# Rows of V for a sparse attention: a gathering engine's indirect DMAs replaced, for four of six query tiles, by copies from register addresses on another queue, and the output stores moved the other way

## The chip, the cores and the metric

The kernel runs on one core of one Trainium2 chip. The metric is the device time of one execution in microseconds (us), median of several runs. A run is put in the state "slow" when it is over 1.5% above the fastest run of the same kernel in its set; such runs are left out of every ratio, and a single run has state "unknown". "Span" is the time from the first to the last instruction of the one execution that the profiler recorded; it is about 2 us shorter than the device time.

The runs fell on several chips, numbered 2, 8, 9 and 10 here. A kernel's ratio is always to the kernel before on the same chip and in the same set; where two sets are set side by side below, it is by their ratios or their traces.

Engines: TensorE (PE in the profile) multiplies matrices, VectorE (DVE) and ScalarE (ACT) do elementwise work, Pool (POOL, GpSimd) issues indirect DMAs and does some gathers itself, and SyncE (SP) mainly issues DMAs. Each takes its instructions in program order, as the queues in the traces below show.

## The reference

A block-sparse attention (768 positions, blocks of 32, 8 heads, 4 batches) followed by a feed-forward stage. Each middle block of queries sees the first and last block, its neighbours, and three sampled blocks.

```python
def _attn_ref(q, k, v, sampled_blocks):
    ...
    mask = np.abs(blk_i - blk_j) <= window          # window = 1
    mask = mask | (blk_i == 0) | (blk_j == 0) | (blk_i == n_blocks - 1) | (blk_j == n_blocks - 1)
    for qb in range(n_blocks):                      # 24 blocks
        for kb in sampled_blocks[qb]:               # 3 of them for each
            mask[qb*block:(qb+1)*block, kb*block:(kb+1)*block] = True
    ...                                             # softmax over the mask, then attn @ v

def _moe_ref(x, w_in, w_out, g_ln):                 # x: 3072 x 512
    h = x @ w_in
    solu = h * softmax(h)                           # (softmax written out in the original)
    ...                                             # layer norm over 1024, times g_ln
    return (ln @ w_out).astype(np.float32)
```

The sampled blocks are data. So the kernel has to fetch, for each block of queries, three blocks of 32 rows of V whose position it learns at run time.

## The kernel before

It works batch by batch, three "tiles" of 256 query rows in each. While batch b is computed, batch b+1 is prepared: V, K and Q are loaded by SyncE, V is cast and written in the order that the gathers want (`place_v`, `write_v`), and the sampled rows are brought in by Pool (`gather_v`). What is prepared when is a table of slots. `at(slot, f)` puts a piece of work in a slot, 24 slots to a batch, and the slots are run in order; since the engines' queues are in order too, a DMA in slot 14 of SyncE goes out behind everything of slots 0 to 13. In particular, what is put in slots 21 to 24 (the second tile's rows) stands ahead of the V loads for the batch after, which begin in slot 24, slot 0 of the next batch.

```python
def load_one(src, b, pr, nm, ...):                  # V, K and Q of one pair of heads
    ...
    nc.sync.dma_start(out=..., in_=src[b, 2*pr : 2*pr+2, :, :]...)      # buffers: kc 3, qc 2, vc 2

def place_v(b, i):                                  # cast to bf16 into vst, on DVE or ACT
    ...
    if b and i % 2:
        nc.scalar.copy(out=dst, in_=src)
    else:
        nc.vector.tensor_copy(out=dst, in_=src)

def near_v(b, t): ...                               # neighbours' rows, two DMAs on SyncE

def gather_v(b, g):                                 # sampled rows of two query blocks
    for i in range(2):
        qb = 2 * g + 1 + i
        nc.gpsimd.indirect_dma_start(               # 96 rows of 1040 bytes
            out=vr[0 : NR * BLK, g, i, :], out_offset=None, in_=v_s[b][:, :],
            in_offset=bass.IndirectOffsetOnAxis(ap=vidx[0 : NR * BLK, qb : qb + 1], axis=0))

def rows_v(t):                                      # 24 row numbers into SyncE registers
    q0, n_ = 8 * t + 1, min(8, NM - 8 * t)
    _, at_row[t] = nc.values_load_multi_w_load_instructions(
        vrow[0:1, :, q0 : q0 + n_], engines=(mybir.EngineType.SP,), ...)

def fetch_v(b, g):                                  # the same rows, 32 at a time, on SyncE
    ...
    for i in range(2):
        for j in range(NR):
            r = at_row[t][j * n_ + 2 * (g - 4 * t) + i]
            nc.sync.dma_start(out=vr[j * BLK : (j + 1) * BLK, g, i, :],
                              in_=v_s[b][bass.ds(r, BLK), :])

def store(b, t, ot):
    ...
        nc.sync.dma_start(out=out[r0 : r0 + n, :], in_=ot[p0 : p0 + n, :])

def plan(b):                                        # what batch b + 1 needs; z = 24 * b
    ...                                             # slots for b > 0:
    #   V loads 0, 2, 4, 6   K loads 1, 3, 5, 7   Q loads 9, 11, 12, 14
    #   place_v 3, 5, 7, 9   K casts 5, 7, 9, 11
    for t in range(NT):
        at(z + (13 + o // 4, 21, 28)[t], lambda t=t: near_v(b + 1, t))
        for g in range(4 * t, min(4 * t + 4, NG)):
            at(z + (13 + o // 4, 21, 28)[t] + g - 4 * t, lambda g=g: gather_v(b + 1, g))
```

`rows_v` and `fetch_v` are already there: batch 0 uses them once, for two of its groups (12 copies). A tile has four groups (the third tile three), a group is one call of `gather_v`, which is two indirect DMAs, or of `fetch_v`, which is six copies. So a batch has 22 indirect DMAs.

The softmax here doesn't subtract the row's maximum and nothing guards it: scores larger than these inputs give would overflow.

## Time and profile before

| | |
|---|---|
| device time, three runs | 277.16 us median (275.26 to 280.33) |
| profiled execution (of another run) | 336.05 us, span 334.3 us |
| PE busy, idle gaps over 0.3 us (profiled) | 259.3 us, 68.9 us |
| of these gaps, inside Pool's bursts of indirect DMAs | 33.7 us of 92 us |
| indirect DMAs on Pool | 76: 10 for batch 0, 22 for each other batch |

The profiled execution and the timed ones disagree by 59 us (336.05 against 277.16). That was the riddle. First, lines of the profile's page. "busy" is in us, with the number of instructions after x; the rows of digits are busy tenths in 40 equal slices of the span, PEclk is the clock granted to TensorE in tenths; then the chain of work that ended last, by engine, and one group of instructions (busy us, mean ns of one, idle before it).

```profile
span 334.3 us, 8508 instructions
...
PE 259.3 (78%) x3646; PEld 172.4 (52%) x3646; DVE 173.2 (52%) x491; ACT 148.3 (44%) x216; POOL 124.3 (37%) x122
...
PE   4974976978296779874859959957967959999984
...
POOL 7053672345757520366660230670670140000000
PEclk9799697699759579996787978996985978999999
...
PE 56%; DVE 17%; issue 9%; another core or an unknown queue 7%; ACT 5%; DMA 4%; ACTq 0%; SPq 0%; DVEq 0%
...
L296 POOL DMA_INDIRECT vr<-v_s_125,vidx x22 | 20.8, 946 | 21.5 <-PE op L533 15.4
```

The span is 334.3 us though PE is busy for only 259.3. Pool's indirect DMAs take 0.95 us each in the profile, and Pool's row of digits shows where they come in long bursts.

Next, the timeline of the kernel before inside one of these bursts (start in us, length, engine, line, operation, out<-in, count, and in brackets the idle time before and its releaser):

```profile
151.78 0.92 POOL L296 DMA_INDIRECT vr<-v_s_125,vidx  x1 [0.30 <-issue]
152.47 0.26 PE L631 MATMUL s3p<-onesf,sq 128*128 128x1 bf16 x4 [1.09 <-issue]
...
153.01 0.92 POOL L296 DMA_INDIRECT vr<-v_s_125,vidx  x1 [0.30 <-issue]
153.89 0.25 PE L631 MATMUL s3p<-onesf,sq 128*128 128x1 bf16 x4 [1.16 <-issue]
...
154.24 0.92 POOL L296 DMA_INDIRECT vr<-v_s_125,vidx  x1 [0.30 <-issue]
```

The columns to look at are the start and the count. Between two indirect DMAs of Pool, 1.23 us apart, PE does four tiny matmuls and then stands still for about a microsecond, with "issue" as releaser: nothing that the profile shows held it. I call this the crawl.

### The profile page before, as it was taken

To read this page: it belongs to the slowest core of one execution; us is meant where nothing else is said; L and a number is where in the kernel's file an instruction comes from. 1 tells how busy PE (TensorE), PEld (TensorE's weight loads), DVE (VectorE), ACT (ScalarE), POOL (GpSimd) and SP (SyncE) were. 2 spreads that over 40 slices of the span, in tenths; PEclk is the share of its full clock that TensorE was granted. 3 is DMA by queue.
4 is the path that set the end of the run, shared out by engine and by line. 5 is a ranking of instruction groups with operands and counts; after the bars stand their busy time and mean duration, and the time that the engine had idled before them with its cause. 6 is when DMAs were issued, how large, how long until landed. Compare 5 with 4: busy or idle time off the path is not lost.

```text
span 334.3 us, 8508 instructions
## 1 busy us (share of the span) xinstructions
PE 259.3 (78%) x3646; PEld 172.4 (52%) x3646; DVE 173.2 (52%) x491; ACT 148.3 (44%) x216; POOL 124.3 (37%) x122
## 2 busy tenths in 40 slices
PE   4974976978296779874859959957967959999984
PEld 1442555556153545762337647635544647677752
DVE  7676436599260335682626418517626416364551
ACT  1662557585131245661316427505514325565332
POOL 7053672345757520366660230670670140000000
PEclk9799697699759579996787978996985978999999
DMA  6799679675305951872183290860240130201011
GB/s 211 269 318 147 202 217 305 221 204 186 85 12 152 269 171 40 285 225 66 43 244 94 74 299 23 266 191 23 81 135 26 56 104 3 65 2 65 2 64 64
DMA packets 29734, 46.03 MB, mean 138 GB/s; under 512 B 4296, under 2 KB 22632, under 8 KB 29696
## 3 DMA queue, kind: packets, MB, share of 16 engines
q1 hardware_dynamic: 24976, 34.75, 32.7%
q0 software_dynamic: 4720, 10.74, 12.4%
q8 instruction: 28, 0.46, 0.6%
q14 instruction: 10, 0.08, 0.1%
HBM read 36.76 MB, written 9.77 MB: 139 GB/s over the span
## 4 chain that ended last, share of the span: by engine, by line
PE 56%; DVE 17%; issue 9%; another core or an unknown queue 7%; ACT 5%; DMA 4%; ACTq 0%; SPq 0%; DVEq 0%
PE h L616 14%; PE ops L657 12%; PE op L533 12%; PE s L410 7%; PE s3p L631 4%; DMA vn_128<-v_s_123 3%; PE tp L340 3%; DVE solu L621 2%; DVE w_out_sb L578 2%; ACT ot L663 2%; PE tps L602 1%; DVE xT L605 1%; DVE qr L333 1%; DMA v_s_123<-vst 1%
## 5 line engine op out<-in xcount | busy, mean ns | idle before, releaser
L616 PE MATMUL h<-xT,w_in_sb 128*128 128x256 bf16 x384 | 60.6, 311 | 7.8 <-DVE solu L621 3.1
L657 PE MATMUL ops<-w_out_sb,solu 128*128 128x512 bf16 x192 | 50.8, 400 | 2.1 <-ACT ot L663 1.8
L621 DVE TENSOR_TENSOR solu<-h,e 128x512 bf16<-128x512 f32 x48 | 33.0, 688 | 32.5 <-ACT e L620 24.2
L616 PEld LDWEIGHTS <-w_in_sb 128*128 128x128 bf16 x384 | 39.5, 109 | 19.3 <-issue 9.5
L620 ACT ACTIVATE e<-h 128x512 bf16<-128x512 f32 x48 | 28.6, 597 | 40.1 <-PE h L616 27.5
L481 DVE RECIPROCAL r<-op 128x4 f32<-128x4 f32 x48 | 8.6, 180 | 57.1 <-PE op L533 19.9
L533 PE MATMUL op<-vr,eb 128*32 128x65 bf16 x640 | 20.5, 206 | 16.0 <-issue 16.0
L533 PEld LDWEIGHTS <-ea 64*64 64x64 bf16 (+1 forms) x496 | 18.3, 109 | 21.3 <-issue 9.3
L296 POOL DMA_INDIRECT vr<-v_s_125,vidx x22 | 20.8, 946 | 21.5 <-PE op L533 15.4
L657 PEld LDWEIGHTS <-solu 128*128 128x128 bf16 x192 | 17.8, 101 | 20.8 <-issue 5.4
L296 POOL DMA_INDIRECT vr<-v_s_126,vidx x22 | 20.5, 931 | 20.3 <-PE op L533 14.2
L412 ACT ACTIVATE eb<-s 128x1024 bf16<-128x1024 f32 (+1 forms) x22 | 20.8, 947 | 15.5 <-remote 10.2
L412 ACT ACTIVATE ea<-s 128x1024 bf16<-128x1024 f32 x22 | 22.5, 1021 | 9.1 <-PE op L533 5.5
L663 ACT ACTIVATE ot<-ops,rs 128x512 f32<-128x512 f32 x24 | 16.3, 688 | 22.9 <-PE ops L657 11.3
L410 PEld LDWEIGHTS <-kT 128*64 128x64 bf16 (+1 forms) x316 | 17.0, 112 | 15.5 <-issue 12.6
L412 ACT ACTIVATE ed<-s 128x768 bf16<-128x768 f32 x16 | 12.8, 811 | 26.0 <-PE op L533 9.2
L296 POOL DMA_INDIRECT vr<-v_s_124,vidx x22 | 21.2, 964 | 8.3 <-issue 6.1
L605 DVE COPY xT<-tps 128x512 bf16<-128x512 bf16 x24 | 9.8, 420 | 25.3 <-PE tps L602 12.4
L533 PEld LDWEIGHTS <-eb 128*32 128x32 bf16 x640 | 11.1, 99 | 22.3 <-issue 20.2
L622 DVE TENSOR_TENSOR sq<-solu 128x512 bf16<-128x512 bf16 x48 | 21.1, 442 | 0.9
L482 DVE TENSOR_TENSOR x<-op,r 128x256 bf16<-128x256 f32 x48 | 20.4, 424 | 1.0
L358 ACT COPY kT<-tp 128x768 bf16<-128x768 bf16 x16 | 12.8, 800 | 14.2 <-PE tp L340 14.1
(292 smaller groups left out, 484.6 us busy)
## 6 DMA issues: line engine op xcount, KB each, us to landing
kc<-in_k_dram SPq DMA_DIRECT2D x16, 384.0 KB
qc<-in_q_dram SPq DMA_DIRECT2D x16, 384.0 KB
out_dram<-ot SPq DMA_DIRECT2D x20, 256.0 KB
vc<-in_v_dram SPq DMA_DIRECT2D x12, 384.0 KB
krt_144<-in_moe_w_out_dram POOLq DMA_DIRECT2D x1, 1536.0 KB
w_in_sb<-in_moe_w_in_dram POOLq DMA_DIRECT2D x1, 1024.0 KB
v_s_123<-vst SPq DMA_DIRECT2D x1, 780.0 KB
vn_128<-v_s_123 SPq DMA_DIRECT2D x1, 780.0 KB
```

The source lines that it names most:

```text
L296: nc.gpsimd.indirect_dma_start(out=vr[0 : NR * BLK, g, i, :], out_offset=None, in_=v_s[b][:, :], in_offset=bass.IndirectOffsetOnAxis(ap=vi ...
L410: nc.tensor.matmul(dst, lhsT, rhs, start=(o % 512 == 0), stop=(x == last[o // 512]), skip_group_check=True)
L412: nc.scalar.activation(out=e, in_=s[:, 0:width], func=ACT.Exp, scale=scale)
L482: nc.vector.tensor_tensor(out=xt[:, :, 2 * pr * D : (2 * pr + 2) * D].rearrange("p a (h d) -> p a h d", h=2), in0=op[:, :, :, 0:D], in1=r. ...
L533: nc.tensor.matmul(o_, l_, r_, start=(x == 0), stop=(x == len(mm) - 1), skip_group_check=True)
L616: nc.tensor.matmul(h[:, ff, :], w_in_sb[:, c, f * P : (f + 1) * P], st["xT"][:, c, :], start=(ff == 0 and c == 0), stop=(ff == 1 and c == ...
L620: nc.scalar.activation(out=st["e"][:, sl, :], in_=h, func=ACT.Exp)
L621: nc.vector.tensor_mul(out=st["solu"][:, sl, :], in0=h, in1=st["e"][:, sl, :])
L622: nc.vector.tensor_mul(out=st["sq"][:, sl, :], in0=st["solu"][:, sl, :], in1=st["solu"][:, sl, :])
L631: nc.tensor.matmul(s3p[:, qt, g : g + 1], st[nm][:, f, qt * P : (qt + 1) * P], onesf[:, 0:1], start=first, stop=(qt == 1 and g == 2 and f ...
L657: nc.tensor.matmul(ops, st["solu"][:, f, qt * P : (qt + 1) * P], w_out_sb[:, f, :], start=(f == 0), stop=(f == KF - 1))
L663: nc.scalar.activation(out=ot, in_=ops, func=ACT.Copy, scale=st["rs"][:, qt : qt + 1])
```

## The change

The intent: take load from Pool. For the first two tiles (of 256 rows, four of 128 rows) of batches 1 to 3, the 16 indirect DMAs are replaced by 48 copies of 32 rows, whose addresses SyncE reads from its registers. To make room on SyncE, the stores of the output go to Pool. The third tile stays with Pool. For batches 2 and 3 the first tile moves one slot later (13 to 14).

```diff
@@ store @@
-            nc.sync.dma_start(out=out[r0 : r0 + n, :], in_=ot[p0 : p0 + n, :])
+            nc.gpsimd.dma_start(out=out[r0 : r0 + n, :], in_=ot[p0 : p0 + n, :])
@@ plan @@
         for t in range(NT):
-            g0 = 4 * t
-            at(z + (13 + o // 4, 21, 28)[t], lambda t=t: near_v(b + 1, t))
+            s0 = z + (14, 21, 28)[t]
+            at(s0, lambda t=t: near_v(b + 1, t))
+            if t < NT - 1:
+                at(s0, lambda t=t: rows_v(t))
             for g in range(4 * t, min(4 * t + 4, NG)):
-                at(z + (13 + o // 4, 21, 28)[t] + g - 4 * t, lambda g=g: gather_v(b + 1, g))
+                at(s0 + g - 4 * t, lambda g=g, f=fetch_v if t < NT - 1 else gather_v:
+                   f(b + 1, g))
```

## The prediction

> **What bounds the kernel now.** The page gives PE 259.3 us busy of a profiled span of 334.3; the timed median is 277.16. So the timed program has room for little more than 18 us of TensorE idleness, if the matmuls take there what they take in the profile. The trace has far more: PE gaps over 0.3 us sum to about 69 us. About 34 us of them lie in the stretches (92 us in all) in which Pool issues the indirect DMAs, where PE does a handful of matmuls every 0.72 us (timeline, 149 to 157 us). I read most of this crawl as something of the profiled run. Timed, the kernel is PE-bound in a lock-step of in-order queues, about 20 us per 256-row tile.
>
> **What the change removes.** Per batch 1 to 3, 16 of 22 indirect DMAs: 1.23 us each with the gap (timeline of Pool), 59 us of Pool time in all. Also 28 store issues of 0.35 us from SyncE, and its waits on ACT's output tiles (168 us in SP's waits, harmless unless a load stands behind one).
>
> **What it adds.** On SyncE, for each of two tiles per batch: one load of 24 registers, 5.09 us the one time the trace has it (212 ns a register; the Trainium skill, "Runtime: NRT & Kernel Launch", section "Instruction fetch mechanics", gives about 200), then 24 copies of 32 rows; the undisturbed ones of batch 0 come every 0.50 us. So 17 us per tile and, with the near rows, 36 us per batch, in order, on the queue that also prefetches Q, K and V. Pool gets 28 stores; its two last direct DMAs took 0.74 and 0.91 us, so about 23 us, and its queue now waits for ACT at each.
>
> **How much is critical.** Pool's gathers seldom are when timed: they end well before their reader. SyncE's new work is. In slot order:
> - Fetching for batch 1: after the staging DMA at 68.6 us, near rows, registers and 12 copies precede the third Q load; it goes out about 7 us later than the 73.7 us of now. Estimated stall 6 to 8 us. The next batch's first V load goes out at about 106 us instead of 101.9, while timed slots run faster: another 5 to 7 us.
> - For batch 2: the last Q load waits for slot 16's relay; only then come 36 us of fetches, ending near slot 30, while V placement of the next batch stands in slot 27 on VectorE. Estimated stall 9 us.
> - For batch 3: no loads behind, nothing lost.
> - Last stores from Pool: 1 to 2 us in the tail.
>
> Cost 20 to 25 us. Against it: what of the crawl is real when timed, and Pool's second K gather coming about 10 us sooner: 0 to 20 us. Balance +8 us: 285 us, 262 to 302. Chances: faster by over 2% 0.33, within 2% 0.17, slower 0.50.
>
> **What would show each step.** In the profile after: six more register loads of 5 us and 144 more copies at 0.5 us on SyncE; Pool busy down by about 35 us; V and Q loads behind the fetches later; VectorE and ACT idle ahead of the V placement and the Q casts, ended by a DMA; smaller PE gaps where the gathers were, so the profiled span may fall even where the timed one rises; stores from Pool at 0.7 to 1.0 us.
>
> **What would make it wrong.** The crawl being real when timed: removing two thirds of the gathers is then worth up to 20 us and the change wins. Copies issued faster than 0.50 us, or slots slower than my 2.5 us, hide the SyncE queue. Copies slowed by other transfers, or Pool's K gathers stuck behind store waits, make it worse than 302.

## The result

The changed kernel took 306.52 us (305.90 to 307.30, four runs), the kernel before 277.44 us (275.26 to 280.33, four runs). The ratio is 1.108, with a 95% interval of 1.100 to 1.115: slower by 11%. Ratios in this document are the mean time of one kernel's fast runs over that of the other's fast runs of the same rounds, so they are not quite the ratio of the medians quoted beside them.

The profile after came from an execution of 306.04 us, of the 275 level. The profile of before, by its span and its crawl, is of the 338 level, so the two must not be subtracted from each other. For that reason the kernel before was profiled once more, on chip 9 (the run c2_before_again below: 275.36 us, span 273.6 us). These are the lines of the page after:

```profile
span 304.2 us, 8906 instructions
...
PE 247.5 (81%) x3628; PEld 168.4 (55%) x3646; DVE 174.6 (57%) x491; ACT 148.2 (49%) x216; POOL 95.6 (31%) x102
...
PE   4885677797868996988899916898989999999880
...
POOL 8033776044452350252413500342240712010102
PEclk9799598669965997997999975697879999999997
...
PE 30%; issue 18%; DVE 17%; DMA 14%; SPq 13%; ACT 4%; POOL 1%; POOLq 0%; ACTq 0%; DVEq 0%
PE ops L657 9%; SPq L314 8%; PE op L533 6%; DMA kc<-in_k_dram 6%; PE h L616 5%; SPq L304 4%; PE s L410 3%; DMA vn_128<-v_s_123 3%; PE tp L340 3%; DMA vr<-v_s_123 2%; DVE solu L621 2%; DVE w_out_sb L578 2%; PE s3p L631 2%; DVE qr L333 2%; DVE sq L622 2%
...
L592 POOL DMA_DIRECT2D out_dram<-ot x28 | 16.0, 572 | 103.0 <-ACT ot L663 103.0
```

And these are the same lines of the kernel before at the same level (with one group more at the end):

```profile
span 273.6 us, 8508 instructions
...
PE 232.7 (85%) x3646; PEld 161.0 (59%) x3646; DVE 172.7 (63%) x491; ACT 147.2 (54%) x216; POOL 124.7 (46%) x122
...
PE   5796495598789859959988999999699999999893
...
POOL 8014577407367567746747662576571700000000
PEclk9799889858999968986999999999999999999998
...
PE 55%; DVE 18%; DMA 12%; issue 4%; ACT 4%; SPq 3%; POOL 2%; ACTq 0%; DVEq 0%
...
L296 POOL DMA_INDIRECT vr<-v_s,vidx x76 | 73.0, 961 | 32.8 <-issue 13.2
...
L410 PE MATMUL s<-qbd,krt 128*128 128x64 bf16 x320 | 15.4, 198 | 2.9 <-POOL krt L380 2.8
```

How to read the pair. Pool's busy time has fallen by 29 us (124.7 to 95.6) while PE's idle time and PE's busy time have both risen: the number of matmuls is the same (the trace after lacks 18 of 3646 records), yet they take 247.5 instead of 232.7 us. The rows of PEclk say why: before, the clock is full (9) almost throughout the second half; after, it dips to 5 and 6 in slices 12 and 13 and again in 25 and 26. And in the chain of work that ended last, SyncE's queue (SPq) has grown from 3% to 13%, of which line 314, the new copies, is 8% and line 304, the register load, 4%.

The same kernel before at the 275 level also explains the riddle. This is its timeline inside a burst of indirect DMAs:

```profile
132.10 0.92 POOL L296 DMA_INDIRECT vr<-v_s,vidx  x1 [0.30 <-PE s L410]
...
132.41 0.34 PE L631 MATMUL s3p<-onesf,e 128*128 128x1 bf16 x8 [0.33 <-DVE solu L621]
...
132.61 0.29 PE L631 MATMUL s3p<-onesf,solu 128*128 128x1 bf16 x6
...
132.76 0.68 PE L410 MATMUL s<-qbd,kT 128*128 128x128 bf16 x9
...
133.33 0.96 POOL L296 DMA_INDIRECT vr<-v_s,vidx  x1 [0.30 <-PE s L410]
```

Pool issues them just as fast as in the first profile (0.92 us, 1.23 us apart; mean 961 ns), but PE does 8, 6 and 9 matmuls in the time in which it did 4. Over all of Pool's bursts (93 us) PE's gaps sum to 7.0 us here, 5.4 of them in the head of the kernel, against 33.7 us at the 338 level. So at the level where the times were taken there was almost nothing to win by taking gathers from Pool.

### Where the 30.6 us come from

Comparing the two executions of the 275 level (spans 273.6 and 304.2 us), PE's idle gaps over 0.3 us grow from 36.6 to 51.4 us (+14.8) and PE's busy time by 14.8 us. Together that is 29.6 of the 30.6 us. Cut at the tiles' first outputs, over half of the loss lies in one stretch, 162.7 to 195.6 us, which takes 32.9 us where the kernel before takes 17.0; each of the eight other stretches compared loses at most 3.3 us. The lines below are of that stretch.

**The idle gaps: loads that come late on SyncE.** This is SyncE's queue in the kernel before at the 275 level, as the V loads of batch 3 are issued (SPq lines give when the issue began and how long it took):

```profile
144.07 0.42 SPq L84 DMA_DIRECT2D vc<-in_v_dram  x1
...
145.05 0.47 SPq L84 DMA_DIRECT2D vc<-in_v_dram  x1
...
159.14 0.39 SPq L84 DMA_DIRECT2D vc<-in_v_dram  x1
...
161.71 0.49 SPq L84 DMA_DIRECT2D vc<-in_v_dram  x1
```

And this is the queue of the changed kernel over the same work:

```profile
163.72 12.37 SPq L314 DMA_DIRECT2D vr<-v_s_125  x24
176.14 1.38 SPq L84 DMA_DIRECT2D vc<-in_v_dram  x1
...
178.08 0.47 SPq L84 DMA_DIRECT2D vc<-in_v_dram  x1
...
181.00 0.39 SPq L84 DMA_DIRECT2D vc<-in_v_dram  x1
...
184.35 0.37 SPq L84 DMA_DIRECT2D vc<-in_v_dram  x1
```

In the changed kernel, 24 copies occupy the queue from 163.7 to 176.1 us, half a microsecond each, and behind them stand the V loads: at 176, 178, 181 and 184 us, against 144, 145, 159 and 162 us before. Ahead of the copies of each tile stands a register load too (4.9 to 5.1 us; register loads are not in this view). Those who needed V had to wait, as the changed kernel's timeline shows of the same moment:

```profile
180.40 0.56 DVE L266 CAST vst<-vc 128x768 bf16<-128x768 f32 x1 [3.82 <-DMA vc<-in_v_dram]
...
181.93 0.82 PE L340 MATMUL tp<-ident,kr 128*128 128x128 bf16 x6 [6.14 <-DVE kr L333]
...
183.49 0.83 ACT L264 CAST vst<-vc 128x768 bf16<-128x768 f32 x1 [6.43 <-DMA vc<-in_v_dram]
...
185.60 0.56 DVE L333 CAST kr<-kc 128x768 bf16<-128x768 f32 x1 [3.72 <-DMA kc<-in_k_dram]
```

VectorE stood for 3.8 and 3.7 us, ScalarE for 6.4 us, each ended by a DMA of V or K. Summed after 60 us, such waits on DMA of VectorE and ScalarE are 2.2 us before and 21.5 us after. PE starves with them: its gap from 175.8 us is 6.1 us long (the second line), until VectorE has cast a K that came late. The stores on Pool make no such wait here: after 60 us no wait over 0.3 us of PE, VectorE or ScalarE in this trace ends with Pool or with an output DMA.

**The busy time: half the clock, for the most part around the stalls.** Below are windows of the kernel before at the 275 level; after the engines' busy times come the granted clock of PE, the share of the DMA engines and GB/s.

```profile
80.00:100.00 20.00, 15.41 (x273) 10.96 (x271) 12.96 (x30) 9.03 (x13) 13.41 (x12) 0.94 0.66 187
...
140.00:160.00 20.00, 18.94 (x303) 13.42 (x302) 13.17 (x33) 11.29 (x18) 12.54 (x13) 1.00 0.60 181
...
180.00:200.00 20.00, 17.00 (x300) 12.40 (x298) 15.15 (x37) 11.41 (x18) 12.89 (x13) 1.00 0.46 137
```

The same windows in the changed kernel:

```profile
80.00:100.00 20.00, 15.46 (x191) 10.63 (x190) 10.57 (x23) 7.26 (x12) 7.68 (x6) 0.66 0.43 117
...
140.00:160.00 20.00, 18.41 (x301) 13.40 (x301) 13.96 (x36) 10.55 (x16) 4.95 (x4) 0.91 0.37 100
...
180.00:200.00 20.00, 14.29 (x173) 8.65 (x174) 7.80 (x25) 9.61 (x12) 4.82 (x4) 0.62 0.79 245
```

In the window 180 to 200 us, which the stall at 175.8 runs into, the clock is 0.62 on average: the trace's records of it show half clock for 17.1 us, from 178.3 to 195.4. The window 80 to 100, in which the late Q loads fall, has 0.66. The clock takes only two values here, 1.0 and 0.5, and changes in steps of about 3.4 us. The Trainium skill, "TensorE: Matmul & The Clock Gate", section "What's actually happening", describes two such states: half of the pulses after an idle window of about 3.4 us, all of them after a busy one. This trace agrees in the two values and in the step, but its half-clock stretches do not begin after idle steps alone: in the step before, PE was busy for 23% (at 178.3 us), but also for 59% (at 86.2 and 209.0), 63% (at 222.7) and 80% (at 140.8), while the clock stayed full after steps of 62% and 63% (from 69.1 and 147.6 us). What decides there was not found.

After 60 us, the kernel before spends 19.0 us at half clock and the changed one 56.5 us; PE is busy in 13.1 and 42.2 us of these. Of the 56.5 us, 34.1 begin with PE's gaps at 85.7 us (1.7 us long), 113.8 (2.6) and 175.8 (6.1); 13.7 us (from 140.8, 209.0 and 222.7) have no gap over 1 us just before them, so not all of it is shown to come from the stalls.

Had the 29.1 us of additional half-clock work taken half as long at full clock, PE's busy time would be 14.5 us lower, which is nearly all of the 14.8 us by which it grew (it grew after 60 us only). That is an estimate from these numbers, of the kind that the section "HAM oscillation — how this bites in real kernels" of the same page makes. It is on the high side: in this trace the matmuls of line 657 start 216 ns apart at full clock and 427 at half, but the small ones of line 533 start 26 and 37 ns apart.

**The tail.** The last lines of the changed kernel:

```profile
295.96 1.27 ACT L663 ACTIVATE ot<-ops,rs 128x512 f32<-128x512 f32 x2
296.94 1.60 POOL L592 DMA_DIRECT2D out_dram<-ot  x3 [9.93 <-ACT ot L663]
```

And those of the kernel before at the same level:

```profile
268.67 1.26 ACT L663 ACTIVATE ot<-ops,rs 128x512 f32<-128x512 f32 x2
269.38 1.57 SPq L592 DMA_DIRECT2D out_dram<-ot  x3
```

In the changed kernel the final stores go out at 297 us and the span ends at 304.2: Pool's program ends with a DRAIN (5.49 us, from 297.9), which the busy times don't count. From the last output tile to the end it takes 7.0 us, the kernel before 3.7; PE's final gap is 7.4 us instead of 4.0.

### The profile page after: what moved, and what is told of

Its sections match the earlier page's. It is cut to its first block, busy times and chain, and to the rows that moved or that the text cites. A ratio compares the mean times of both kernels' runs of the same rounds, so it can differ in the third digit from the quotient of the medians.

```text
span 304.2 us, 8906 instructions
## 1 busy us (share of the span) xinstructions
PE 247.5 (81%) x3628; PEld 168.4 (55%) x3646; DVE 174.6 (57%) x491; ACT 148.2 (49%) x216; POOL 95.6 (31%) x102
## 4 chain that ended last, share of the span: by engine, by line
PE 30%; issue 18%; DVE 17%; DMA 14%; SPq 13%; ACT 4%; POOL 1%; POOLq 0%; ACTq 0%; DVEq 0%
PE ops L657 9%; SPq L314 8%; PE op L533 6%; DMA kc<-in_k_dram 6%; PE h L616 5%; SPq L304 4%; PE s L410 3%; DMA vn_128<-v_s_123 3%; PE tp L340 3%; DMA vr<-v_s_123 2%; DVE solu L621 2%; DVE w_out_sb L578 2%; PE s3p L631 2%; DVE qr L333 2%; DVE sq L622 2%
## 5 line engine op out<-in xcount | busy, mean ns | idle before, releaser
L616 PE MATMUL h<-xT,w_in_sb 128*128 128x256 bf16 x384 | 51.7, 281 | 2.6 <-DVE xT L605 1.5
L592 POOL DMA_DIRECT2D out_dram<-ot x28 | 16.0, 572 | 103.0 <-ACT ot L663 103.0
L616 PEld LDWEIGHTS <-w_in_sb 128*128 128x128 bf16 x384 | 35.8, 100 | 9.7 <-issue 3.3
L657 PEld LDWEIGHTS <-solu 128*128 128x128 bf16 x192 | 19.1, 107 | 21.2 <-issue 7.9
L340 PE MATMUL tp<-ident,kr 128*128 128x128 bf16 x96 | 10.0, 254 | 24.5 <-DVE kr L333 23.7
L622 DVE TENSOR_TENSOR sq<-solu 128x512 bf16<-128x512 bf16 x48 | 22.1, 460 | 1.2
L340 PEld LDWEIGHTS <-kr 128*128 128x128 bf16 x96 | 7.0, 112 | 28.2 <-DVE kr L333 26.2
L410 PEld LDWEIGHTS <-kT 128*64 128x64 bf16 (+1 forms) x316 | 16.5, 113 | 10.9 <-issue 7.8
L605 DVE COPY xT<-tps 128x512 bf16<-128x512 bf16 x24 | 9.5, 418 | 13.7 <-PE tps L602 13.6
L533 PE MATMUL op<-vr,eb 128*32 128x65 bf16 x640 | 17.2, 208 | 0.0
L678 PE MATMUL warm<-ident 128*128 128x512 bf16 x42 | 15.2, 471 | 1.5 <-POOL ident L101 1.5
```

The source lines that it names most:

```text
L340: nc.tensor.matmul(tp[:, r, :], c[:, r, :, :].rearrange("p h d -> p (h d)"), ident, is_transpose=True, start=(r == 0), stop=(r == R6 - 1))
L410: nc.tensor.matmul(dst, lhsT, rhs, start=(o % 512 == 0), stop=(x == last[o // 512]), skip_group_check=True)
L533: nc.tensor.matmul(o_, l_, r_, start=(x == 0), stop=(x == len(mm) - 1), skip_group_check=True)
L616: nc.tensor.matmul(h[:, ff, :], w_in_sb[:, c, f * P : (f + 1) * P], st["xT"][:, c, :], start=(ff == 0 and c == 0), stop=(ff == 1 and c == ...
L622: nc.vector.tensor_mul(out=st["sq"][:, sl, :], in0=st["solu"][:, sl, :], in1=st["solu"][:, sl, :])
L657: nc.tensor.matmul(ops, st["solu"][:, f, qt * P : (qt + 1) * P], w_out_sb[:, f, :], start=(f == 0), stop=(f == KF - 1))
```

## The experiments

The theories that the runs were to tell apart:

- **Queue**: the copies and register loads hold SyncE's in-order queue, and V, K and Q loads behind them come late.
- **Stores**: output stores in Pool's queue make Pool's K gathers and indirect DMAs late, or end the kernel later.
- **Traffic**: the copies themselves load the DMA engines (the small rows) and slow other transfers.
- **Crawl**: indirect DMAs on Pool slow TensorE; taking them away is a gain that offsets part of the cost.

The tables of times give the median of all runs of a kernel and its ratio to the kernel before in the same set.

| run | chip, level | us | ratio to before, 95% |
|---|---|---|---|
| c0_before_again | 2, 338 | 346.7 (one run; set median 337.7) | – |
| e1_stores_pool | 2, 338 | 346.5 | 1.031 (1.024–1.037) |
| e2_fetch_only | 2, 338 | 319.0 | 0.947 (0.940–0.954) |
| e3_sync_busy | 2, 338 | 362.5 | 1.079 (1.069–1.088) |
| a1_after_again | 9, 275 | 303.8 | 1.105 (1.098–1.111) |
| e5_vkq_first | 9, 275 | 295.6 | 1.081 (1.074–1.088) |
| e6_rows_once | 9, 275 | 293.3 | 1.073 (1.065–1.082) |
| e7_one_tile | 9, 275 | 285.5 (fast runs 282.1, 283.1) | none given |
| f1_stores_pool | 10, 338 | 344.1 | 1.019 (1.011–1.028) |
| f3_sync_busy | 10, 338 | 363.8 | 1.073 (1.062–1.085) |
| e8_first_and_once | 10, 338 | 301.6 | 0.895 (0.886–0.904) |
| e9_tail_sync | 10, 338 | 315.4 | 0.937 (0.928–0.946) |
| c2_before_again | 9, 275 | 275.4 (one run) | – |
| g3_sync_busy | 9, 275 | 301.0 | 1.107 (1.093–1.121) |
| e10_all_three | 9, 275 | 281.7 | 1.030 (1.021–1.039) |
| h1_thin_copies | 8, 338 | 322.0 | 0.944 (0.931–0.956) |
| h2_stores_pool | 8, 338 | 344.0 | 1.012 (1.004–1.020) |
| e11_one_tile_mended | 8, 338 | 317.5 | 0.927 (0.916–0.938) |

### The kernel before, again (c0_before_again; c2_before_again)

No edit. On chip 2:

> The kernel before, unchanged, profiled once more: is the crawl in its first profile (334.3 us of span against 277 timed) a property of the kernel or of that one profiled execution? If profiling this kernel slows it, the span is again 320 to 345 us with TensorE gaps of some 60 to 70 us bunched where Pool issues its indirect DMAs. If the first profile was a chance, the span is 272 to 282 us and the gaps sum to less than 35 us.

Measured: 346.7 us, and the eleven other runs of the kernel before in this set, only timed, took 334 to 361 us. PE's gaps sum to 72.0 us, 35.6 of them in Pool's bursts. So the profiler does not make the long time: executions without it are as long. This overturned my reading of the first profile. On chip 9:

> The kernel before, for its profile. If the chip is of the fast level (274 to 285 us): TensorE gaps over 0.3 us sum to less than 40 us, and in the stretches in which Pool issues indirect DMAs they take less than a fifth of the time, where the slow level has 36 to 39 per cent. If the fast level has the same crawl, the level has another cause. If the chip is slow: as before, 335 to 347 us.

Measured: 275.4 us, span 273.6, with the crawl almost absent (lines above). The level goes with the chip in all that was run: the sets on chips 2, 8 and 10 have it at 333 us or more, the two sets on chip 9 and the first timings at 270 to 286. What makes TensorE crawl there was not found; with one set on each of these chips, a cause that goes with the time of a set rather than with its chip is not excluded. Between the two levels (334.3 and 273.6 us of span), PE's gaps differ by 32 us, 27 of them in the bursts, and PE's busy time by 27 us. Most of the latter is the clock again: half-clock windows are 96 us in all at the 338 level and 33 us at the other, PE is busy in 72 and 26 us of them, and half of the difference, by the same estimate as above, is 23 us.

### The stores alone (e1, f1, h2_stores_pool)

```diff
 # the kernel before, with only this:
-            nc.sync.dma_start(out=out[r0 : r0 + n, :], in_=ot[p0 : p0 + n, :])
+            nc.gpsimd.dma_start(out=out[r0 : r0 + n, :], in_=ot[p0 : p0 + n, :])
```

> Only the second part of the change: stores issued by Pool, all gathers as before. SyncE theory (the loss comes from SyncE's in-order queue being filled with register loads and copies): within 2 per cent of before, 275 to 282 us, with 1 to 3 us from the last stores landing later. Rival (Pool, waiting for ACT at each store, holds back its K gathers and the remaining indirect DMAs): at least half of the loss appears here, 290 us or more.

> Stores alone on Pool once more, hoping for a chip where before takes 274 to 280 us. SyncE theory: only the tail shows, 7 us (10.9 us from last tile to end against 3.9, as the first run of it had), so 281 to 287 us at the fast level, with the other 20 us of the loss absent. Rival (Pool behind store waits): 293 us or more. At the slow level: 1.03 of before again.

> Stores alone on Pool, third time, for the fast level. Theory: only the tail, 10.9 us from the last output tile to the end instead of 3.9, so 280 to 284 us and a ratio of 1.02 to 1.03. If Pool's order behind store waits costs more: 288 us or above. At the slow level: 342 to 348 us again.

Measured: 1.031, 1.019 and 1.012, all at the 338 level. Stores on Pool, with all of its gathers left there, cost 1 to 3%, 4 to 10 us. The tail alone is 7 us: from the last output tile to the end of the span e1 takes 10.9 us, the kernel before 3.85. At the 275 level the stores alone were never measured. In mid-kernel the trace of the changed kernel shows no wait of an engine for them (above), so they can have cost little there; the tail is theirs for certain (see e9).

### The fetches alone (e2_fetch_only)

```diff
 # the changed kernel, with only this undone:
-            nc.gpsimd.dma_start(out=out[r0 : r0 + n, :], in_=ot[p0 : p0 + n, :])
+            nc.sync.dma_start(out=out[r0 : r0 + n, :], in_=ot[p0 : p0 + n, :])
```

> Only the first part of the change: V rows fetched by SyncE, stores left on SyncE. SyncE theory: as slow as the full change or slower, 303 to 318 us, because the store waits and 28 more issues stand in the same queue. Rival (stores on Pool make the loss): below 290 us.

Measured: 319.0 us, 0.947. At the 338 level the fetches win 5%. The remaining indirect DMAs still crawl: 16.1 us of PE gaps in 33.8 us of bursts, against 35.6 us for all of them in c0. So the crawl is a real cost at that level and was partly removed. This edit was not run at the 275 level; the changed kernel, which has the same fetches, loses 10% there (a1), where there is next to no crawl to remove.

### SyncE held without fetching (e3, f3, g3_sync_busy)

```diff
 # the changed kernel, with all rows gathered by Pool again, and in place of the fetches:
+            if t < NT - 1:
+                at(s0, lambda: busy(24))          # load 24 registers, then one copy of 32 bytes
             for g in range(4 * t, min(4 * t + 4, NG)):
-                at(s0 + g - 4 * t, ...fetch_v if t < NT - 1 else gather_v...)
+                at(s0 + g - 4 * t, lambda g=g: gather_v(b + 1, g))
+                if t < NT - 1:
+                    at(s0 + g - 4 * t, lambda: busy(12))
```

> The change with every V row gathered by indirect DMA again, but SyncE kept busy for the same time at the same places of its queue (about 17.8 us per tile: registers loaded 24 and then four times 12, each with one copy of 32 bytes to a scratch row so that the load is kept). No extra traffic worth the name. SyncE theory (time in the queue alone, not what the copies do): 298 to 312 us, with V and Q loads going out as late as in the change. Rival (the 144 copies of 32 rows disturb the loads, PE or the memory by their traffic): 276 to 286 us.

> SyncE kept busy with register loads and no copies once more, hoping for a chip where before takes 274 to 280 us. SyncE theory: as slow as the change apart from the tail, which has 10.9 instead of 7.0 us: 302 to 312 us at the fast level. Rival (the copies' traffic): 281 to 288 us, no slower than the stores alone.

> SyncE kept busy with register loads, no copies. At the fast level, SyncE theory: 302 to 312 us (the change's stalls, and the tail of 76 indirect DMAs, 10.9 us instead of 7.0); rival (the copies' traffic makes the loss): 281 to 288 us. At the slow level: 361 to 366 us, as twice before.

Measured: 1.079, 1.073 (338 level) and 1.107 (275 level). It looks like the queue theory's number, but I don't count it, since the experiment missed its aim. The register loads were of contiguous numbers, and these turned out to be three times cheaper than the strided ones of the changed kernel: at the median 1.62 us for 24 and 0.75 us for 12, not 5 us. So SyncE was held for only 8 to 9 us per tile, about half, and in g3 the V loads of batch 2 began at 89.5 us, earlier than in the kernel before. (Those of batch 3 came late, at 160.5 to 176.8 us, but no engine is shown to wait for them.) The loss of g3 came from elsewhere: 10.9 us in the tail (with all the gathers and the stores on Pool), a wait of 7.9 us of ScalarE for an output tile whose store stood in Pool's queue behind gathers, and half-clock windows after it. So g3 says nothing certain of SyncE. But two pairs can be compared: e3 and f3 are e1 and f1 with SyncE held, and the first tile of two batches a slot later. They took 16 and 20 us more on the same chips (362.5 against 346.5, 363.8 against 344.1). So even half of the holding, without a copy of rows, goes with a loss of some 5% at the 338 level. The largest new gap of PE is 10.1 us at 84.5 us in e3 and 9.1 us at 83.8 in f3, ahead of the cast of a Q; the cause of this wait was not taken apart.

### The changed kernel again (a1_after_again)

> The change itself, on whichever chip comes up. The runs so far show the kernel before at two levels: 275 to 280 us where the change was first timed, 334 to 342 us on the chip of the last four runs, where TensorE crawls during Pool's indirect DMAs. SyncE theory: if before is at 275 to 280 here, the change is again at 304 to 309 us (ratio 1.10); if before is at 334 to 342, the change removes two thirds of the crawl and is faster, 308 to 325 us (ratio 0.92 to 0.96). Rival (the level is the chip's general speed): the ratio is about 1.10 at either level, so 370 us at the slow one.

Measured: 303.8 us, 1.105 against the kernel before on the same chip 9. The result repeats. So do the stalls: V loads of batch 3 at 176.4 to 184.8 us, PE gap of 5.4 us at 177.4.

### Loads ahead of the copies (e5_vkq_first)

```diff
 # the changed kernel, with the first two V and K loads of batches 2 and 3, and the Q loads of batch 1, ahead of copies
+            early = -4 if b and i < 2 else None
-            at(z + slots["V"][i], lambda i=i: load_v(b + 1, i))
-            at(z + slots["K"][i], lambda i=i: load_k(n0 + i))
+            at(z + (early or slots["V"][i]), lambda i=i: load_v(b + 1, i))
+            at(z + (early or slots["K"][i]), lambda i=i: load_k(n0 + i))
 ...
-                at(s0 + g - 4 * t, ...)
+                at(18 + g // 2 if b == 0 and t == 0 else s0 + g - 4 * t, ...)
```

> The change with SyncE's queue in another order: the first two V and K loads of the next batch go before the second tile's fetches (slot 20 instead of 24 to 27), and the third and fourth Q loads of batch 1 before the first tile's copies. Same instructions, same traffic. SyncE theory: most of what the change loses comes back, 15 to 25 us below the change on the same chip; at the fast level 281 to 291 us. Rival (the amount of SyncE work or the copies' traffic costs, wherever it stands): within 5 us of the change.

Measured: 295.6 us, 8 us less than the changed kernel in the same set. The order of a queue was changed and no work or traffic was taken away, so the order itself costs, as the queue theory says. But 8 us is about half of the 15 to 25 expected: the stall was moved as much as removed. SyncE's queue in this run:

```profile
163.74 13.32 SPq L314 DMA_DIRECT2D vr<-v_s  x24
...
178.09 0.39 SPq L84 DMA_DIRECT2D vc<-in_v_dram  x1
```

The first two V loads now go out before the copies. The third, for which there is no buffer earlier (two of `vc`), goes out at 178.1 us, and PE has a gap of 8.0 us at 175.1.

### Registers loaded once (e6_rows_once)

```diff
-                at(s0, lambda t=t: rows_v(t))
+                at(s0, lambda t=t: t in at_row or rows_v(t))
```

> The change with the row numbers loaded into registers once per tile position instead of once per batch: five of the six loads of 5.1 us are gone from SyncE, all copies stay. SyncE theory: the second batch's chain of fetches is 10 us shorter and the first's 5 us, so 8 to 15 us below the change on the same chip; at the fast level 292 to 299 us. Rival (register loads sit in SyncE's idle time): within 3 us of the change.

Measured: 293.3 us, 10.5 us less than the changed kernel (9.9 us by the fast runs alone). The row numbers are the same for all batches, so five of the seven loads of 5 us can go. The V loads of batch 3 come at 165.8 to 176.0 us and the gaps over 2 us after the head are gone except in the tail. Nothing but SyncE's time for register loads was removed: 25 us of it gave 10 us of the kernel's.

### One tile instead of two (e7_one_tile)

```diff
-            if t < NT - 1:
+            if t < 1:
...          f=fetch_v if t < 1 else gather_v
```

> Half of the change: SyncE fetches only the first 256-row tile of each batch, the second is gathered by indirect DMA again. SyncE theory: the next batch's V loads no longer stand behind 18 us of a second tile, only the third and fourth Q loads of batch 1 are late: at the fast level 284 to 292 us, 14 to 22 us below the change. At the slow level the crawl of the second tile comes back and offsets part of it: within 8 us of the change. Rival (cost per copy): half of the loss remains, 291 to 293 us at the fast level.

Measured: 285.5 us median, of which two runs, 282.1 and 283.1, are fast; the fast runs of the kernel before in this set were 273.7 to 276.7. The V loads are back in their place (the first of batch 2 at 91.1 us). What is left is, for the most part, the tail, which is longer than with two tiles: 9.0 us from the last output tile to the end, against 3.7 before: 5.3 of the 8 us between the fast runs' means.

### Loads ahead and registers once (e8_first_and_once)

The edits of e5 and e6 together.

> Both mendings of SyncE's queue together: next batch's first two V and K loads and the third and fourth Q load ahead of the copies, and the row numbers loaded once. Alone they gave 295.6 and 293.3 us where the change gave 303.8 and before 278.8; with the loads first, the stall had moved to the third V load, which waited for the end of the second tile's copies (8.0 us of TensorE gap at 175 us). SyncE theory: that load now comes 10 us earlier, the stall is gone, 280 to 286 us at before's fast level; what remains over before is the tail. If the copies' traffic or count matters by itself: 288 us or more.

Measured on chip 10: 301.6 us, 0.895. At the 338 level this version beats the kernel before by 10.5%, and has the lowest ratio of all that was run there.

### The last stores on SyncE (e9_tail_sync)

```diff
-            nc.gpsimd.dma_start(out=out[r0 : r0 + n, :], in_=ot[p0 : p0 + n, :])
+            (nc.sync if b == B - 1 else nc.gpsimd).dma_start(
+                out=out[r0 : r0 + n, :], in_=ot[p0 : p0 + n, :])
```

> The change with the stores of the last batch back on SyncE, which is idle by then. In the change 7.0 us pass from the last output tile to the end of the span, 5.5 of them in a drain of Pool that starts with its last store; before had 3.9. Theory of the tail: the distance goes back to 3.4 to 3.9 us and the time falls by 3 to 4 us, to 299 to 301 at the fast level. Rival (the end waits for the data of the last stores, not for Pool): within 1 us of the change.

Measured on chip 10: 315.4 us, 0.937. The final gap of PE is 4.1 us instead of 7.4: the tail is repaired, by 3.3 us. The trace records of Pool's DRAIN give the cause: it takes 5.49 us in the changed kernel (28 indirect DMAs), 7.45 us in e7 (52) and 9.41 us in e1 (76), that is 0.082 us more for each. With the stores on SyncE, Pool's last work is an indirect DMA long before the end (272 us of 334 in the first profile), and its DRAIN runs hidden (10.8 us from 214.6 us in c2, begun while the last indirect DMAs were still being issued). Stores on Pool put the DRAIN behind the last output tile.

### All three repairs (e10_all_three)

The edits of e5, e6 and e9 together.

> The change with all three mendings: loads ahead of the copies, registers loaded once, last batch's stores on SyncE. SyncE theory: at the fast level 276 to 283 us, within 2 per cent of before, since the stalls and the tail were all that the change cost; at the slow level 295 to 300 us against about 337 of before, faster than before and than the change. If something else of the change costs: 286 us or more at the fast level.

Measured on chip 9: 281.7 us, 1.030 (1.021 to 1.039). The three repairs change only the order of SyncE's queue, the number of register loads and the queue of the last seven stores. They bring the loss from 10.5% down to 3%, some 21 of 29 us, a little less than expected (within 2% of before). The profile (of a slow run, 285.1 us) still has a gap of 3.8 us at 171.5, where the third V load goes out at 170.5, and windows at half clock. That may be the rest, with the other stores on Pool; it was not taken apart further. So no version that was run beats the kernel before at the 275 level.

### Thin copies (h1_thin_copies)

A wrong kernel (relative error 0.51): each of the copies of batches 1 to 3 moves 16 of 520 columns, 3% of the bytes, with as many issues.

```diff
+                w_ = 16 if b else HE
-                nc.sync.dma_start(out=vr[..., g, i, :],    in_=v_s[b][bass.ds(r, BLK), :])
+                nc.sync.dma_start(out=vr[..., g, i, 0:w_], in_=v_s[b][bass.ds(r, BLK), 0:w_])
+    nc.gpsimd.memset(vr[0 : NR * BLK, 0:4, :, :], 0.0)        # once, in the head
```

> The change with each of the 144 new copies cut to the first 16 of its 520 columns: the same instructions and register loads on SyncE, 3 per cent of their bytes. The result is wrong on purpose. SyncE theory: V and Q loads go out as late as in the change and the time stays at 300 to 308 us at the fast level (slow level: 312 to 322). Rival (the bytes of the copies slow the loads or other engines): 285 us or less at the fast level.

Measured on chip 8: 322.0 us, 0.944 (e9, which has the shorter tail but all bytes, had 0.937 on chip 10). SyncE's queue in this run:

```profile
175.31 13.78 SPq L315 DMA_DIRECT2D vr<-v_s  x24
189.14 0.42 SPq L84 DMA_DIRECT2D vc<-in_v_dram  x1
```

24 copies hold it for 13.8 us as the full ones do (12.4 us in the changed kernel), the V load stands behind them as before, ScalarE waits 5.4 us in all for V, and PE has a gap of 5.2 us at 190.3. The stretch between two tiles' outputs is 35.9 us, in e9 35.1. Taking away 97% of the bytes helped nothing in this stretch. The cost of the copies is their issue, not their bytes. (Each copy still moves 32 rows, so a cost for each row is not excluded by this run. The memset takes 3.9 us in the head, so the total time is no measure here. The run is of the 338 level; at the 275 level it was not made.)

### One tile, mended (e11_one_tile_mended)

One tile as in e7, registers loaded once as in e6, the Q loads of batch 1 ahead as in e5, the last stores on SyncE as in e9.

> One tile per batch fetched by SyncE, its registers loaded once, the Q loads ahead of the copies, the last batch's stores on SyncE. The plain one-tile version took 282 to 283 us in its fast runs with a tail of 9.0 us. Theory: the tail goes to under 5 us and the late Q loads are mended, 274 to 279 us at the fast level, equal to before within 2 per cent; at the slow level 310 to 322 us, faster than before. If it is 282 us or more at the fast level, the fetching costs something that is not yet found.

Measured on chip 8: 317.5 us, 0.927. At the 338 level it wins less than e8. It leaves 61.8 us of gather bursts, 15.6 of them gaps, against e8's 33.2 and 11.2; that is 4.4 us of PE gaps, so most of the difference in the ratios (0.927 and 0.895) is not explained by it. Whether it is above or below 275 us at the other level stays open.

## Why the prediction was wrong

The direction had the larger chance, 0.50 for slower, but 285 us and the range up to 302 were wrong: it was 306.5.

1. **"What of the crawl is real when timed, and Pool's second K gather coming about 10 us sooner: 0 to 20 us" is the step that failed.** With a cost of 20 to 25 us and a balance of +8, it counted about 14 us of gain. At the level where the times were taken there was almost nothing to gain: the kernel before loses there 7.0 us of 93 to gaps in Pool's bursts, 5.4 of them in the head, which the change does not touch. And PE's idle time put down to Pool's K gather is 2.8 us in all (the last line of the page at the 275 level); the second K gather for batch 1 did come sooner, at 84.5 us instead of 91.6, and that wait is gone, but it could not pay more. So 4.4 us of PE's idle time stood in the place of 14, which is 10 us or more of the 21 by which the prediction missed. With no gain at all its own cost would have given 297 to 302 us; the rest is point 4.
2. "I read most of this crawl as something of the profiled run" was right in its use and wrong in its cause. By their times it is absent from the runs that were timed first, but not because they had no profiler: on three chips every run that was only timed is as long as the profiled one or within some per cent of it. Having the time of 277 us and a trace of 334 us, the prediction should have drawn the conclusion from its own sentence, that a crawl which is not in the times can't be won back in the times. It gave the gain term the middle of its range instead. Its "What would make it wrong" looked for the danger on the other side, a crawl that is real when timed.
3. The mechanism of the cost was right. SyncE got 36 us of work a batch (predicted), by register loads of 4.9 to 5.1 us and copies of 0.50 us at the median, 0.56 on average. The third and fourth Q loads of batch 1 went from 72.7 and 75.1 us to 82.5 and 86.0 (predicted: about 81 for the third). The first V load of batch 2 went to 110.5 us (predicted about 106 instead of 101.9; at this level it went out at 90.8 before, so the delay was 20 us and not 4), and the largest stall is the placement of V for batch 3 on VectorE and ScalarE. e5 and e6 recover 8 and 10 of some 29 us by touching the queue alone, e10, with the last stores moved too, some 21, and h1 shows the largest stall unchanged when the bytes are taken away.
4. The size of the cost, "20 to 25 us", was too small: about 30. It priced the stalls as idle time. The idle gaps did grow by less than that (14.8 us, with the tail), but PE also worked longer at half clock, for the most part around the stalls, which the prediction left out altogether: an estimated 14.5 us, on the high side.
5. "Last stores from Pool: 1 to 2 us in the tail" was 3.4 us in PE's final gap. Not the stores are slow (0.57 us each, where 0.7 to 1.0 was predicted), but Pool's DRAIN is exposed behind them.
6. Pool busy "down by about 35 us" was 29. "The profiled span may fall even where the timed one rises" came true, 334.3 to 304.2 us, for a reason other than the one given: the two profiles are, by their spans, of different levels. That was luck.

What stays open: why chips differ in the crawl; what the stores alone cost at the 275 level; what the last 3% of e10 are made of; what halves the clock after steps in which PE is more than half busy; where e3 and f3 lose what they lose over e1 and f1; and the changed kernel itself was never run at the 338 level (e9, its nearest there, gained 6%).

## What to carry to other kernels

Before moving work from one in-order queue to another, write down what stands behind it there: forty-eight small copies and two register loads a batch cost more here, at the 275 level, as a delay of the prefetches behind them than the gathers cost on a queue with nobody waiting (at the 338 level the fetches alone won 5%), and a stall of 6.1 us was followed by 17.1 us at half clock. If the profile and the times of a kernel differ by a fifth, first get a trace and a time from the same execution, since a gain that only the other one shows is no gain. And before an engine is given the last stores, look at what it does when it closes.

## What the Trainium skill lacked or had wrong

- "Runtime: NRT & Kernel Launch", section "Instruction fetch mechanics", gives about 200 ns for each register "even for bulk". A strided load (3 rows of 8 numbers) agrees: 5.09 us for 24, 212 ns each. Contiguous numbers do not: at the median 1.62 us for 24 and 0.75 us for 12, that is 67 and 63 ns each (e3_sync_busy). The page speaks of registers loaded from HBM, and the table here lies in SBUF, so the page lacks this case rather than being shown wrong.
- "DMA: Bandwidth & Descriptors", section "Issuing engines are not separate DMA queues", says that issuing from several engines saves only the sequencer's time to issue, "which is usually small relative to the DMA itself". It does not say that this time also delays whatever stands behind: here 24 copies of 32 rows hold SyncE for 12.4 us, and for 13.8 us with 3% of the bytes, and the order of that queue was worth 8 us (e5) of the kernel. How long the copies themselves take to land was not measured.
- No section of "TensorE: Matmul & The Clock Gate" says how busy a window has to be for the clock to stay full. Here half clock began after steps in which PE was busy for 59, 63 and 80%, and did not begin after others of 62 and 63%.
- No page that I read has the DRAIN at the end of Pool's program growing with the indirect DMAs issued: 5.49, 7.45 and 9.41 us after 28, 52 and 76 of them (after, e7, e1, all with output stores last), 0.082 us for each.
- No page that I read has chips on which TensorE crawls while Pool's indirect DMAs are being issued: the same kernel took about 275 us on chip 9 and about 338 us on chips 2, 8 and 10, with PE gaps of 7.0 us (c2, chip 9) and 35.6 us (c0, chip 2) in its bursts of indirect DMAs. That the chip is the cause was not shown.
